# Soft-capped attention with a three-way max MLP: smaller token block, PSUM order, first loads and weight conversions changed

## The chip, the cores and the metric

The kernel runs on one core of a Trainium2 chip. The metric is the device time of one execution in microseconds; the time of the kernel before is the median of three runs. All rows below come from one further execution, recorded by the profiler.

## What is computed

Attention over 4 batches, 12 heads, 448 tokens and a head size of 64, with scores capped by a tanh, then an MLP over the 1792 tokens: three products with 768 x 768 matrices, their elementwise maximum, and a product with a fourth. All is float32; the reference, cut to its core:

```
def _attn_ref(q, k, v, cap):
    scale = 1.0 / np.sqrt(q.shape[-1])
    scores = scale * np.matmul(q, k.transpose(0, 1, 3, 2))
    scores = cap * np.tanh(scores / cap)
    scores = scores - np.max(scores, axis=-1, keepdims=True)
    attn = np.exp(scores)
    attn = attn / (np.sum(attn, axis=-1, keepdims=True) + 1e-09)
    return np.matmul(attn, v)

def _moe_ref(x, w1, w2, w3, w_out):
    h = np.maximum(np.maximum(x @ w1, x @ w2), x @ w3)
    return h @ w_out
```

## The kernel before

**Attention.** One group is four heads of one batch, so there are 12 groups, t = 0 to 11, and `step` is run for each of them and once more (t = 12) for what is left of the last. A group has 7 blocks of 64 keys, j = 0 to 6. For each block `scores` (L126) multiplies keys and queries into one of the two PSUM tiles `qk`, `tanh` (L132) and `expo` (L135) run on ScalarE into `e_all`, and `values` (L140) accumulates into PSUM tile `av`. With a cap of at most 40 no maximum is subtracted. The row sums are made by `add` on VectorE (s_t) and `sums` (L154) on TensorE into PSUM tile `sm`; `recip` (L161 to L164), `normalize` and `split_x` (L176, L177) on VectorE divide and write the result as a high and a low part into `xx`. A step begins with the sums of the group before it and ends with the first scores of the next one. All code stands in the order in which each engine runs it (a manual schedule); `FILL`, `CONV`, `SCALED` and `LOADS` say which extra work goes into which step.

**Weights.** The weights come as the 64-bit words of the host. Each of the 24 column strips n (18 of the first layer, three matrices for each of 6 output strips, and 6 of the second) is loaded by `conv_load` into `wd` and turned by the six operations of `conv` into a high and a low part, `wh` and `wl`. `CONV` names, by step, pairs of strip and operation that VectorE runs at the end of the step; `SCALED` names a step in which operation 0 is done by ScalarE; `LOADS` names the step in which a strip is loaded, by SP's queue.

**The MLP.** The tokens are cut into blocks, b = 0 of 256 tokens (`REST`) and b = 1 to 3 of 512. A unit (n, b) is one strip times one block: for each of 6 groups of 128 input features high x high, high x low and low x high are added up in one PSUM bank. For b = 0 the high weights take both parts of the 256 tokens in one product of 512 columns (L234), and a product of 256 columns adds the low weights (L235); `empty` then copies one half of the bank by ScalarE (L255) and adds the other by VectorE, and for the second and third matrix a further VectorE operation takes the maximum. For b = 1 to 3 three products of 512 columns are used (L239 to L241), and the bank is emptied by one operation. Eight units, those of `FILL`, stand inside the attention steps 4 to 11, in the bank `sm[:, 0]`: (0, 0), (1, 0), (2, 0) in steps 4, 5 and 6, then five with 512 tokens. The rest is done by `mlp` behind the attention, n by n and b by b. When the last strip of the first layer (n = 17) has been done for a block, `split_h` cuts the hidden values of this block into a high part (ScalarE, L276) and a low part (VectorE). `mlp` takes PSUM banks from the list `banks` in turn; the two halves of one PSUM tile are two banks. A strip has four units, so all its units of one parity are in `qk`, and all of the next strip's in `sm` and `av`:

```
banks = [t[:, i, :] for a, b in ((qk[0], qk[1]), (sm, av)) for i in range(2) for t in (a, b)]
```

**The start.** ScalarE's queue issues the cap (L441) and the first half of q (L443), SP's queue the first part of k, the second half of q, the rest of k, v and the first weights (L442 to L445, `load_v`, `conv_load`). Nine products of zeros (L450, `WARM`) run on TensorE meanwhile. The cap gives the scale of the tanh and a flag, on which all engines branch.

## Time and profile before

| | |
|---|---|
| median of 3 runs | 516.14 us (515.65 to 517.76) |
| profiled execution | 516.17 us |
| its span | 514.4 us |
| TensorE busy | 495.9 us, 96% of the span, 3073 products |
| VectorE, ScalarE busy | 269.0 us (52%), 233.3 us (45%) |
| steps 0 to 3 | to 61 us |
| steps 4 to 12 | 61 to 187 us |
| MLP behind the attention | 187 to 509.6 us |

The share of a busy engine over the whole span hides that different engines set the pace in different stages; so the profile is read stage by stage, and the row at which an engine starts again after a wait names what ended the wait. In the profile PE is TensorE, PEld its weight loads, DVE is VectorE, ACT is ScalarE, and a q behind a name is the engine's queue. L104 is a helper for VectorE's two-operand operations, so these are told apart by their tiles. A row of busy times gives the stretch and its length in us, then for PE, PEld, DVE, ACT and POOL the busy us and the instructions, then the granted TensorE clock as a share of 2.4 GHz, the busy share of the DMA engines and GB/s. A row of a timeline gives start and duration in us, engine, line, operation, tiles, shape and count; in brackets the idle time before it and what ended it.

### The profile page before, as it was taken

The numbers are of one execution on the slowest core, as the hardware profiler recorded it, in microseconds if no ns is written. First come the engines' busy times: TensorE is split into PE (matmuls) and PEld (weight loads), VectorE is DVE, ScalarE is ACT, GpSimd is POOL, SyncE is SP. The second block draws the span as 40 slices with busy tenths as digits, with TensorE's granted clock in tenths as the row PEclk, the third lists the DMA queues.
The fourth block names the chain that finished last, engine by engine and source line by source line (L and its number), as shares of the span: only waits on it lengthen the run. The fifth ranks groups of instructions, "written<-read, shape, count | busy, mean of one in ns | idle before, by whom it ended". The sixth has DMA issues, their size and how long they took to land.

```text
span 514.4 us, 7208 instructions
## 1 busy us (share of the span) xinstructions
PE 495.9 (96%) x3073; PEld 344.5 (67%) x3073; DVE 269.0 (52%) x355; ACT 233.3 (45%) x298; POOL 0.4 (0%) x6
## 2 busy tenths in 40 slices
PE   6899999989999999999999999999999997999996
PEld 3333344444455558888888888888888886888884
DVE  1798999986778963434324414423432585223100
ACT  5999999979788721311211121021022462222211
POOL 0000000000000000000000000000000000000000
PEclk9999999999999999999999999999999998999999
DMA  8234333412232100301301111210130101333111
GB/s 303 106 108 171 108 108 108 148 58 90 91 108 98 62 1 0 124 19 44 122 1 61 62 61 62 62 61 6 57 124 0 63 0 51 128 118 134 52 72 67
DMA packets 12710, 41.42 MB, mean 81 GB/s; under 512 B 1536, under 2 KB 2944, under 8 KB 12672
## 3 DMA queue, kind: packets, MB, share of 16 engines
q1 hardware_dynamic: 12240, 40.54, 22.8%
q8 instruction: 26, 0.43, 0.3%
q10 hardware_dynamic: 432, 0.36, 0.2%
q14 instruction: 12, 0.10, 0.1%
HBM read 35.39 MB, written 5.51 MB: 80 GB/s over the span
## 4 chain that ended last, share of the span: by engine, by line
PE 80%; DVE 10%; ACT 7%; issue 2%; DMA 1%; ACTq 0%; DVEq 0%
PE qk L239 9%; PE qk L240 9%; PE qk L241 9%; PE av L140 6%; PE qk L126 6%; PE av L239 6%; PE av L240 6%; PE av L241 6%; PE sm L239 4%; PE sm L241 4%; PE sm L240 4%; PE sm L234 4%; ACT e_all L132 3%; DVE s_t L104 3%; ACT e_all L135 3%; DVE xx L104 2%
## 5 line engine op out<-in xcount | busy, mean ns | idle before, releaser
L132 ACT ACTIVATE e_all<-qk,sc_t 128x896 f32<-128x896 f32 x84 | 83.3, 1006 | 13.1 <-PE qk L126 12.6
L135 ACT ACTIVATE e_all<-e_all,acap 128x896 f32<-128x896 f32 x84 | 86.5, 1046 | 0.5
L126 PE MATMUL qk<-q_t,k_t 64*64 64x448 f32 x672 | 78.6, 543 | 7.2 <-ACT e_all L132 6.1
L239 PE MATMUL qk<-xx,wh 128*128 128x512 f32 x204 | 80.4, 394 | 2.9 <-DVE q_t L104 2.9
L240 PE MATMUL qk<-xx,wh 128*128 128x512 f32 x204 | 80.0, 392 | 0.0
L241 PE MATMUL qk<-xx,wl 128*128 128x512 f32 x204 | 79.9, 392 | 0.0
L140 PE MATMUL av<-e_all,v_t 64*64 64x448 f32 x672 | 74.9, 536 | 0.3 <-DVE x_t L104 0.3
L104 DVE TENSOR_TENSOR s_t<-s_t,e_all 128x896 f32<-128x896 f32 x55 | 59.8, 1087 | 10.0 <-ACT e_all L135 7.7
L223 ACT CAST wh<-cw 128x768 fp32r<-128x768 f32 x21 | 17.6, 836 | 88.5 <-DVE cw L219 88.5
L126 PEld LDWEIGHTS qk<-q_t,k_t 64*64 64x64 f32 x672 | 23.4, 132 | 47.6 <-issue 24.1
L239 PE MATMUL av<-xx,wh 128*128 128x512 f32 x132 | 51.4, 390 | 0.0
L241 PE MATMUL av<-xx,wl 128*128 128x512 f32 x132 | 51.4, 389 | 0.0
L240 PE MATMUL av<-xx,wh 128*128 128x512 f32 x132 | 51.3, 389 | 0.0
L140 PEld LDWEIGHTS av<-e_all,v_t 64*64 64x64 f32 x672 | 25.4, 133 | 38.3 <-issue 35.4
L104 DVE TENSOR_TENSOR wl<-cw,wh 128x768 fp32r<-128x768 f32 x24 | 22.9, 955 | 47.3 <-ACT wh L223 39.8
L239 PEld LDWEIGHTS qk<-xx,wh 128*128 128x128 f32 x204 | 38.6, 189 | 12.2 <-DVE q_t L104 3.3
L241 PEld LDWEIGHTS qk<-xx,wl 128*128 128x128 f32 x204 | 38.7, 190 | 8.3
L240 PEld LDWEIGHTS qk<-xx,wh 128*128 128x128 f32 x204 | 38.7, 190 | 7.6
L239 PE MATMUL sm<-xx,wh 128*128 128x512 f32 x96 | 38.0, 395 | 0.0
L241 PE MATMUL sm<-xx,wl 128*128 128x512 f32 x96 | 37.4, 390 | 0.0
L240 PE MATMUL sm<-xx,wh 128*128 128x512 f32 x96 | 37.4, 389 | 0.0
L104 DVE TENSOR_TENSOR e_all<-e_all,qk 128x512 f32<-128x512 f32 (+1 forms) x17 | 11.2, 657 | 38.8 <-PE qk L241 36.8
(94 smaller groups left out, 552.1 us busy)
## 6 DMA issues: line engine op xcount, KB each, us to landing
wd<-in_wts_dram SPq DMA_DIRECT2D x24, 768.0 KB, 4.4
v_t<-in_v_dram SPq DMA_DIRECT2D x12, 448.0 KB, 3.3
k_t<-in_k_dram SPq DMA_DIRECT2D x11, 448.0 KB, 3.4
q_t<-in_q_dram SPq DMA_DIRECT2D x11, 448.0 KB, 4.7
out_dram<-q_t SPq DMA_DIRECT2D x6, 256.0 KB, 2.0
out_dram<-s_t SPq DMA_DIRECT2D x6, 256.0 KB, 2.0
out_dram<-x_t SPq DMA_DIRECT2D x5, 256.0 KB, 2.0
out_dram<-x_t SPq DMA_DIRECT2D x3, 128.0 KB, 2.2
```

What stands on the lines that cost most here:

```text
L104: eng.tensor_tensor(out=out, in0=in0, in1=in1, op=op)
L126: nc.tensor.matmul(ps[rows(s), R, 0:S], k_t[t % 2][rows(R), j, s, :], q_t[t % 2][rows(R), s, :], start=True, stop=True, skip_group_check=True,
L132: nc.scalar.activation(out=e_of(t, j), in_=slot(t, j)[:, :, 0:S], func=AF.Tanh, scale=sc_t)
L135: nc.scalar.activation(out=e_of(t, j), in_=e_of(t, j), func=AF.Exp, scale=acap)
L140: nc.tensor.matmul(av[rows(R), s, 0:S], v_t[t % 2][rows(s), j, R, :], e_of(t, j)[rows(s), R, :], start=(j == 0), stop=(j == NJ - 1), skip_ ...
L223: nc.scalar.copy(out=h, in_=d)
L234: nc.tensor.matmul(ps, w_h, xx[:, :, kc, at], start=(kc == 0), stop=False, skip_group_check=True)
L239: nc.tensor.matmul(ps, w_h, a_h, start=(kc == 0), stop=False)
L240: nc.tensor.matmul(ps, w_h, a_l, start=False, stop=False)
L241: nc.tensor.matmul(ps, w_l, a_h, start=False, stop=(kc == KC - 1))
```

## The change

- A unit of the 256-token block is made of three products of 256 columns, as the other blocks are of three of 512; both parts of `empty` for b = 0 become one operation: a copy by ScalarE for the first matrix and for the output, a maximum on VectorE for the second and third. The buffers `l_t` go.
- `banks` names the four PSUM tiles in turn, first their first halves, then their second.
- The conversions of the strips 0 to 2 move: those of one step are now in the step before it, or split in another way, the operation that ScalarE did in step 4 is done by VectorE in step 3, and strip 2 is loaded in step 1.
- The cap is stored as a column behind the first group's q. One load on ScalarE's queue brings both; behind it on the same queue come the rest of k, v and the first weights. SP's queue keeps the first part of k.
- Seven products of zeros stand at the start.

```diff
...
 CAP_LO = 1e-6
-WARM = 9
+WARM = 7
...
 BY_PE = (0, 1, 2, 3, 11)
-CONV = {1: [(0, 4), (0, 5)], 2: [(1, 0), (1, 1)], 3: [(1, 2), (1, 3)], 4: [(1, 4), (1, 5), (2, 1)],
-        5: [(2, 2), (2, 3), (2, 4), (2, 5)], 9: [(3, 1)], 10: [(3, 2), (3, 3)]}
-SCALED = {4: 2, 9: 3}
-LOADS = {0: 1, 2: 2, 6: 3, 11: 4}
+CONV = {0: [(0, 4), (0, 5)], 1: [(1, 0), (1, 1)], 2: [(1, 2), (1, 3)], 3: [(1, 4), (1, 5), (2, 0)],
+        4: [(2, 1), (2, 2)], 5: [(2, 3), (2, 4), (2, 5)], 9: [(3, 1)], 10: [(3, 2), (3, 3)]}
+SCALED = {9: 3}
+LOADS = {0: 1, 1: 2, 6: 3, 11: 4}
...
 @with_exitstack
-def attn_max_mlp_kernel(ctx: ExitStack, tc: tile.TileContext, q, k, v, cap, wts, out):
-
+def attn_max_mlp_kernel(ctx: ExitStack, tc: tile.TileContext, first, q, k, v, wts, out):
...
-    cap_t, acap, sc_t, eps_f, eps_g, fl = (
-        tl(n, [128, 1]) for n in ("cap_t", "acap", "sc_t", "eps_f", "eps_g", "fl")
-    )
+    acap, sc_t, eps_f, eps_g, fl = (tl(n, [128, 1]) for n in ("acap", "sc_t", "eps_f", "eps_g", "fl"))
     fl_i = tl("fl_i", [128, 1], I32)
...
-    q_t = ring("q_t", 2, [128, 2, S])
+    q_0 = tl("q_0", [128, 2 * S + 8])
+    q_t = [q_0[:, 0:2 * S].rearrange("p (a b) -> p a b", a=2), tl("q_1", [128, 2, S])]
+    cap_t = q_0[:, 2 * S:2 * S + 1]
     k_t = ring("k_t", 2, [128, NJ, 2, 64])
...
     m_0 = tl("m_0", [128, TOK])
-    l_t = ring("l_t", 2, [128, REST])
     wd = ring("wd", 2, [128, KC * 128, 2], I32)
...
     o_t = [flat(t)[:, 0:512] for t in (*q_t, *s_t, *x_t)]
-    banks = [t[:, i, :] for a, b in ((qk[0], qk[1]), (sm, av)) for i in range(2) for t in (a, b)]
+    banks = [t[:, i, :] for i in range(2) for t in (qk[0], qk[1], sm, av)]
...
         nc.sync.dma_start(out=quarters(k_t[t % 2]), in_=k[t])
-        nc.sync.dma_start(out=flat(q_t[t % 2]), in_=q[t])
-
-    def load_v(t):
-        nc.sync.dma_start(out=quarters(v_t[t % 2]), in_=v[t])
+        nc.sync.dma_start(out=flat(q_t[t % 2]), in_=q[t - 1])
+
+    def load_v(t, queue=nc.sync):
+        queue.dma_start(out=quarters(v_t[t % 2]), in_=v[t])
...
-    def conv_load(n):
-        nc.sync.dma_start(out=flat(wd[n % 2]), in_=wts[n].bitcast(I32))
+    def conv_load(n, queue=nc.sync):
+        queue.dma_start(out=flat(wd[n % 2]), in_=wts[n].bitcast(I32))
...
         at = slice(*BLOCKS[b])
+        ps = ps[:, 0:at.stop - at.start]
         for kc in kcs:
             w_h, w_l, a_h, a_l = wh[n % 3][:, kc, :], wl[n % 3][:, kc, :], xx[:, 0, kc, at], xx[:, 1, kc, at]
-            if b == 0:
-                nc.tensor.matmul(ps, w_h, xx[:, :, kc, at], start=(kc == 0), stop=False, skip_group_check=True)
-                nc.tensor.matmul(
-                    ps[:, 0:REST], w_l, a_h, start=False, stop=(kc == KC - 1), skip_group_check=True
-                )
-                continue
             nc.tensor.matmul(ps, w_h, a_h, start=(kc == 0), stop=False)
...
         at = slice(*BLOCKS[b])
-        if n >= 3 * KC:
-            dst = out[n - 3 * KC][:, at]
-            o = o_t[outs[0] % len(o_t)][:, 0:dst.shape[1]]
-            outs[0] += 1
-        else:
-            o = m_t[f][:, at] if w == 0 else l_t[n % 2]
-        if b == 0:
-            nc.scalar.copy(out=o, in_=ps[:, 0:REST])
-            tt(nc.vector, o, o, ps[:, REST:2 * REST], ALU.add)
-            if n < 3 * KC and w:
-                tt(nc.vector, m_t[f][:, at], m_t[f][:, at], o, ALU.max)
-        elif n < 3 * KC and w:
-            tt(nc.vector, m_t[f][:, at], m_t[f][:, at], ps, ALU.max)
-        elif (n, b) == (NU - 1, NB - 1):
+        ps = ps[:, 0:at.stop - at.start]
+        if n < 3 * KC:
+            m = m_t[f][:, at]
+            if w == 0:
+                nc.scalar.copy(out=m, in_=ps)
+            else:
+                tt(nc.vector, m, m, ps, ALU.max)
+            return
+        dst = out[n - 3 * KC][:, at]
+        o = o_t[outs[0] % len(o_t)][:, 0:at.stop - at.start]
+        outs[0] += 1
+        if (n, b) == (NU - 1, NB - 1):
             one, two = slice(0, 256), slice(256, 512)
...
             nc.scalar.dma_start(out=dst[:, two], in_=o[:, two])
-            return
         else:
             nc.scalar.copy(out=o, in_=ps)
-        if n >= 3 * KC:
             nc.sync.dma_start(out=dst, in_=o)
...
     with tc.manual_schedule():
-        nc.scalar.dma_start(out=cap_t, in_=cap.partition_broadcast(128))
         nc.sync.dma_start(out=k_t[0][:, 0:2].rearrange("p a b c -> p (a b c)"), in_=k[0, :, 0:256])
-        nc.scalar.dma_start(out=q_t[0][:, 0], in_=q[0, :, 0:S])
-        nc.sync.dma_start(out=q_t[0][:, 1], in_=q[0, :, S:2 * S])
-        nc.sync.dma_start(out=k_t[0][:, 2:].rearrange("p a b c -> p (a b c)"), in_=k[0, :, 256:])
-        load_v(0)
-        conv_load(0)
+        nc.scalar.dma_start(out=q_0[:, 0:2 * S + 1], in_=first)
+        nc.scalar.dma_start(out=k_t[0][:, 2:].rearrange("p a b c -> p (a b c)"), in_=k[0, :, 256:])
+        load_v(0, nc.scalar)
+        conv_load(0, nc.scalar)
         nc.vector.memset(wz.bitcast(F32), 0.0)
...
-_INS = ["q", "k", "v", "cap", "wts"]
+_INS = ["first", "q", "k", "v", "wts"]
...
     host = {
-        "q": qq.reshape(NG, 128, 2 * S),
+        "first": _np.concatenate(
+            [qq[0, 0].reshape(128, 2 * S), _np.broadcast_to(_np.asarray(inputs["cap"]).reshape(1, 1), (128, 1))], axis=1
+        ),
+        "q": qq.reshape(NG, 128, 2 * S)[1:],
         "k": kk.reshape(NG, 128, 2 * S),
         "v": vv.reshape(NG, 128, 2 * S),
-        "cap": _np.asarray(inputs["cap"]).reshape(1),
         "wts": _np.concatenate([w_in.reshape(18, 128, KC * 128), w_out.reshape(6, 128, KC * 128)]).view(_np.int64),
...
```

What the order of instructions becomes is shown at three places. ScalarE at its start (DMA rows are the loads that its queue issues), before:

```order
L441 DMA cap_t_61<-in_cap_dram 128x1
L443 DMA q_t0_70<-in_q_dram 128x448
L453 ACT_TABLE_LOAD
L453 ACTIVATE acap_62<-cap_t_61 128x1
L460 ACTIVATE eps_f_64<-acap_62 128x1
L132 ACTIVATE e_all_76<-qk0_100,sc_t_63 128x896
```

And after:

```order
L431 DMA q_0_69<-in_first_dram 128x897
L432 DMA k_t0_71<-in_k_dram 128x640
L112 DMA v_t0_73<-in_v_dram 128x896
L198 DMA wd0_84<-in_wts_dram 128x1536
L440 ACT_TABLE_LOAD
L440 ACTIVATE acap_61<-q_0_69 128x1
L447 ACTIVATE eps_f_63<-acap_61 128x1
L130 ACTIVATE e_all_75<-qk0_97,sc_t_62 128x896
```

The load of q stands first, with the cap in it, and three loads that SP's queue had issued stand behind it, ahead of the table load.

VectorE from the unit of step 5 to the sums of step 6 (s_t is the running sum of exponents, x_t the reciprocal, cw, wh and wl belong to the conversion, m_0 is the running maximum of the MLP), before:

```order
L104 TENSOR_TENSOR l_t1_86<-l_t1_86,sm_102 128x256
L104 TENSOR_TENSOR m_0_84<-m_0_84,l_t1_86 128x256
L104 TENSOR_TENSOR s_t1_78<-s_t1_78,e_all_76 128x896 x4
L215 SCALAR_TENSOR_TENSOR cw0_89<-wd0_87,cw0_89 128x768
L219 SCALAR_TENSOR_TENSOR cw0_89<-wd0_87,cw0_89 128x768
L225 CAST wh2_93<-cw0_89 128x768
L104 TENSOR_TENSOR wl2_96<-cw0_89,wh2_93 128x768
L161 STREAM_TRANSPOSE x_t1_80<-sm_102 128x896
```

And after:

```order
L102 TENSOR_TENSOR m_0_83<-m_0_83,sm_99 128x256
L102 TENSOR_TENSOR s_t1_77<-s_t1_77,e_all_75 128x896 x4
L217 SCALAR_TENSOR_TENSOR cw0_86<-wd0_84,cw0_86 128x768
L223 CAST wh2_90<-cw0_86 128x768
L102 TENSOR_TENSOR wl2_93<-cw0_86,wh2_90 128x768
L159 STREAM_TRANSPOSE x_t1_79<-sm_99 128x896
```

Two operations are gone ahead of the reciprocal of step 6: the add that joined the two halves of the unit, and one step of the conversion, which now stands a step earlier.

TensorE at the start of the second layer, the last three products of unit (18, 1) and the first three of (18, 2), with the semaphores that each waits for (Activation is ScalarE; xx holds the hidden values), before:

```order
L239 MATMUL qk1_101<-xx_83,wh0_91 128x512 [waits Activation_49]
L240 MATMUL qk1_101<-xx_83,wh0_91 128x512 [waits DVE_49]
L241 MATMUL qk1_101<-xx_83,wl0_94 128x512
L239 MATMUL qk0_100<-xx_83,wh0_91 128x512 [waits DVE_49]
L240 MATMUL qk0_100<-xx_83,wh0_91 128x512
L241 MATMUL qk0_100<-xx_83,wl0_94 128x512
```

And after:

```order
L232 MATMUL qk1_98<-xx_82,wh0_88 128x512 [waits Activation_49]
L233 MATMUL qk1_98<-xx_82,wh0_88 128x512 [waits DVE_49]
L234 MATMUL qk1_98<-xx_82,wl0_91 128x512
L232 MATMUL sm_99<-xx_82,wh0_88 128x512 [waits DVE_49,Activation_49]
L233 MATMUL sm_99<-xx_82,wh0_88 128x512 [waits DVE_49]
L234 MATMUL sm_99<-xx_82,wl0_91 128x512
```

Unit (18, 2) goes to `sm` and not back to `qk0`; its products wait one by one for the parts of xx, where before one wait at its head stood for all of them.

## Rows read from the trace of the kernel before

**Rows 1.** Busy time by stretch: step 3, step 6, the MLP.

```profile
47.95:61.00 13.05, 12.28 (x136) 4.73 (x132) 11.64 (x15) 12.92 (x16) 0.00 (x0) 1.00 0.33 110
...
89.84:106.05 16.21, 14.21 (x132) 6.13 (x132) 15.64 (x19) 15.38 (x18) 0.00 (x0) 1.00 0.38 134
...
186.65:514.40 327.75, 320.07 (x1462) 265.94 (x1458) 118.22 (x174) 70.86 (x120) 0.00 (x0) 0.99 0.18 61
```

**Rows 2.** TensorE's timeline, steps 5 and 6: start, duration, instruction, wait.

```profile
75.60 0.93 PE L154 MATMUL sm<-s_t,ones 64*64 64x448 f32 x8
...
88.59 0.97 PE L126 MATMUL qk<-q_t,k_t 64*64 64x448 f32 x8
89.84 0.98 PE L154 MATMUL sm<-s_t,ones 64*64 64x448 f32 x8 [0.28 <-DVE s_t L104]
...
106.05 0.98 PE L154 MATMUL sm<-s_t,ones 64*64 64x448 f32 x8 [1.73 <-DVE s_t L104]
```

**Rows 3.** TensorE's timeline at the start of the second layer.

```profile
418.51 0.39 PE L234 MATMUL qk<-xx,wh 128*128 128x512 f32 x1
...
424.48 0.39 PE L241 MATMUL qk<-xx,wl 128*128 128x512 f32 x1
427.77 0.50 PE L239 MATMUL qk<-xx,wh 128*128 128x512 f32 x1 [2.90 <-DVE q_t L104]
...
433.59 0.39 PE L239 MATMUL qk<-xx,wh 128*128 128x512 f32 x1
```

**Rows 4.** Busy time by stretch as in rows 1, one microsecond behind the hole.

```profile
430.00:431.00 1.00, 1.00 (x4) 0.81 (x3) 0.18 (x1) 0.00 (x0) 0.00 (x0) 0.50 0.00 0
```

**Rows 5.** VectorE's timeline, the low halves of block 3.

```profile
424.30 3.09 DVE L104 TENSOR_TENSOR xx<-e_all,xx 128x512 fp32r<-128x512 f32 x5
```

**Rows 6.** Instruction groups by form: count, busy us, mean ns, idle.

```profile
L104 DVE TENSOR_TENSOR wl<-cw,wh 128x768 fp32r<-128x768 f32 x24 | 22.9, 955 | 47.3 <-ACT wh L223 39.8 <-PE qk L241 7.5
L215 DVE SCALAR_TENSOR_TENSOR cw<-wd,cw 128x768 int32<-128x768 int32 x24 | 22.9, 955 | 0.3
...
L225 DVE CAST wh<-cw 128x768 fp32r<-128x768 f32 x3 | 1.7, 555 | 0.0
```

**Rows 7.** VectorE's timeline, emptying the unit of step 5.

```profile
84.39 0.41 DVE L104 TENSOR_TENSOR l_t<-l_t,sm 128x256 f32<-128x256 f32 x1
```

**Rows 8.** VectorE's timeline, the reciprocal at the start of step 4.

```profile
62.70 1.12 DVE L161 STREAM_TRANSPOSE x_t<-sm 128x896 f32<-128x896 f32 x1 [0.23 <-PE sm L154]
```

**Rows 9.** TensorE's timeline, unit (17, 0) and the next one's start.

```profile
404.15 0.39 PE L234 MATMUL sm<-xx,wh 128*128 128x512 f32 x1
404.38 0.28 PE L235 MATMUL sm<-xx,wl 128*128 128x256 f32 x1
404.49 0.40 PE L234 MATMUL sm<-xx,wh 128*128 128x512 f32 x1
...
406.26 0.40 PE L239 MATMUL av<-xx,wh 128*128 128x512 f32 x1
```

**Rows 10.** Timeline of the weight loads in unit (0, 0).

```profile
67.01 0.19 PEld L234 LDWEIGHTS sm<-xx,wh 128*128 128x128 f32 x1
...
67.12 0.19 PEld L235 LDWEIGHTS sm<-xx,wl 128*128 128x128 f32 x1
```

**Rows 11.** Timeline of all engines at the start.

```profile
0.73 0.41 ACTq L441 DMA_DIRECT2D cap_t<-in_cap_dram  x1
...
1.17 0.45 ACTq L443 DMA_DIRECT2D q_t<-in_q_dram  x1
...
1.38 3.73 PE L450 MATMUL sm<-wz 128*128 128x448 f32 x9 [1.38 <-DVE wz L448]
...
6.16 1.73 PE L126 MATMUL qk<-q_t,k_t 64*64 64x448 f32 x16 [1.05 <-DMA q_t<-in_q_dram]
```

**Rows 12.** Loads by issue: engine, count, KB each, us from issue to landing.

```profile
q_t<-in_q_dram ACTq DMA_DIRECT2D x1, 224.0 KB, 4.9
...
cap_t<-in_cap_dram ACTq DMA_DIRECT2D x1, 0.5 KB, 3.6
```

## The prediction, made before the changed kernel ran

> **What bounds the kernel now.** I read the busy times by stretch first, to learn which engine each stage waits for, then the timeline of that engine where the stage is longer than its work. Three regimes show. In the first attention steps (t = 0 to 3) ScalarE is busy all the time, 12.92 of 13.05 us in step 3, and VectorE has slack (11.64 us) [rows 1]. In steps 4 to 6 a first-layer unit is put into each step and VectorE fills up, 15.64 of 16.21 us in step 6 [rows 1]. From step 7 on TensorE runs without a gap, and in the MLP it is busy for 320.07 of 327.75 us [rows 1]; what it lacks there is one hole and the tail after its last product.
>
> The loss in steps 5 and 6 is read from where the row sums of one step follow those of the next [rows 2]. Step 5 starts its sums at 75.60; its last score group starts at 88.59, and the sums could follow 0.80 later, so a step with nothing missing takes 88.59 + 0.80 - 75.60 = 13.79 us. It took 14.24, the next one 106.05 - 89.84 = 16.21. Both times the releaser is VectorE's s_t: 0.45 + 2.42 = 2.87 us lost.
>
> The hole in the MLP lies where the second layer begins [rows 3]. The last product before it starts at 424.48, its successor could start 0.23 later, at 424.71, and starts at 427.77, released by VectorE's q_t. That is the add that empties unit (18, 0), out of PSUM tile qk0; the waiting unit (18, 2) takes the other half of the same tile. After the hole the granted clock falls to 0.50, the 1.2 GHz level [rows 4]. Unit (18, 3) starts at 433.59; without the hole it would have been 424.71 + 18 x 0.2269 = 428.79 (a unit is 18 products; from 406.26 to 418.51 three units run, 12.25 / 54 = 0.2269) [rows 3, 9]. The loss is 4.80 us, idle time and slow clock together.
>
> **The change part by part.** The sum is made against the profiled execution, 516.17 us, whose span is 514.4; the median of the runs shown is 516.14, so the same sum serves both.
>
> *Four PSUM tiles in turn.* In the new order of banks a unit meets its tile again four units later, not two. Unit (18, 2) then takes sm, last used by (17, 2), and (18, 0) is emptied by ScalarE alone. What it still waits for are its own inputs, the split halves of block 2; VectorE is at the last five low halves of block 3 from 424.30 on, so those of block 2 are done before that [rows 5]. What is late next is unit (18, 3): its last low half ends at 424.30 + 3.09 = 427.39, and TensorE would be there at 428.79, a margin of 1.40 us. So the hole closes and, with no idle time ahead of it, I expect no slow clock: **4.8 us gained**; between 4.0, if the margin is eaten in part, and 4.8.
>
> *VectorE in steps 4 to 6.* Conversion steps move forward by one step. Step 4 gives away a cast (0.555) and a low half (0.955) and gets one of 0.955 back: 0.56 less. Step 5 gives away 0.96 [rows 6]. Emptying a 256-token unit costs VectorE an add of 0.41 and, for the units of steps 5 and 6, a max of like length before [rows 7]; the new form is nothing for the unit of step 4 (a copy by ScalarE alone, 0.41 less) and one max for those of steps 5 and 6 (0.41 less each). In all 0.56 + 0.41 + 0.96 + 0.41 + 0.41 = 2.75 us of VectorE's work leave three steps in which it has no gaps. Part of the 0.97 of step 4 only becomes a wait, since there the last exponent comes just ahead of the add. The lower bound is 1.78 (steps 5 and 6 alone), the upper the 2.87 that TensorE lost; I take about the middle, **2.35 us**, which leaves TensorE about half a us short of closing the gap in step 6. ScalarE also loses the conversion of step 4 and two copies; it is not late there, so that is worth nothing by itself.
>
> *Where the conversions go.* Steps 0 to 3 are ScalarE's; VectorE's fullest of them is step 3. The tightest place is the start of step 4: VectorE waits 0.23 us for the sums there [rows 8], and the conversions ahead of that wait grow from 2 x 0.955 to 0.955 + 0.555 + a scaling that I put at the cast's 0.555, by 0.16 us. That fits and costs nothing; with the cover gone it would be 0.16. Moving the load of weight 2 a step forward puts 768 KB ahead of the next k and q on SP's queue; both have their first reader a whole step later. Nothing.
>
> *Three products of 256 columns.* Per 128 input features the old pair takes (406.26 - 404.15) / 6 = 0.352 us; in the six pairs the product of 512 columns holds the engine for 0.23 to 0.24 us, mean 0.235, and that of 256 for 0.11 to 0.12, mean 0.117 [rows 9]. The new form is three of 256: 3 x 0.117 = 0.351. The doubtful part is the weight load, now three where there were two. The record of one is 0.19 us long, longer than the product, but two of them start 0.11 apart [rows 10], so they overlap, and the 0.117 already holds a product whose successor loads its own weights meanwhile. No row shows three in succession. If the cost of a column is what the 512-column products show (0.2269 / 512 x 256 = 0.1135), three are 0.340; if all of their excess over 512 columns at 2.4 GHz (0.2269 - 0.2133 = 0.0136) is paid by each product, 0.361. Over 24 units x 6 groups that is from 1.6 us gained to 1.3 lost; I take the 0.351, the nearest row, **0.1 us gained**.
>
> *The start.* The queue of ScalarE carries the cap before the first half of q, so q is issued at 1.17 and lands 4.9 us later; the scores start at 6.16 [rows 11, 12]. In the new order q with the cap as its last column is issued first, at 0.73, and k's first part is the only other load that the first scores need; the rest follows on ScalarE's queue behind q. The nearest rows bound the landing: the cap alone took 3.6 us from 0.73, so 4.33, and q's own 4.9 gives 5.6 [rows 12]. I take 5.0, between them, since fewer bytes are ahead of q than before: scores at 5.15, **1.0 us gained**, from 0.45 to 1.7. The scale for the first tanh needs a few tiny VectorE operations behind the cap; they run beside the first scores. Steps 0 to 3 are ScalarE's without a gap, so this moves everything behind it.
> By the rows alone that is a choice between two ends, and a rule speaks for the poorer one. The Trainium skill ("Trainium Kernel Development and Optimization", Key Constraints) says that all queues share the same 16 DMA engines and that issuing from several engines saves only issue time. By it the start gives just the 0.45 us, and the sum would end at 508.5.
>
> The two warm-up products taken out are off the path as long as q lands after the others. They run 0.41 us apart, 3.73 for nine [rows 11], for 448 columns, a slower pace than the 0.227 of 512 columns later. If with seven the first scores still run at that pace, the first 8 take 1.5 instead of 0.75 us: up to 0.75 lost, taken at nothing.
>
> The sum: 4.8 + 2.35 + 0.1 + 1.0 = 8.25 us; 516.17 - 8.25 = **507.9 us**.
>
> **The rivals.** *The weight loads set the pace (slower than before).* If three products of 256 in succession each need the full 0.19 us of a weight load, a group is 0.57 instead of 0.352, 144 times: 31 us lost, against 8.15 gained elsewhere: 539 us. It would decide from a product of (0.352 + 8.15 / 144) / 3 = 0.136 us on. For it speaks the length of the record, and that in the old pair the mean distance of two loads is 0.176, not far below it. Against it: two of three overlap by 0.08 us in every pair without falling behind. Chance 0.05.
>
> *The hole stays under another name.* If unit (18, 2) or (18, 3) waits for its halves, or for an emptying that the new order makes late, as long as it did for qk0, the 4.8 is not gained: 512.7 us. For it: VectorE is busy throughout this place. Against it: the halves are done 1.4 us before TensorE comes. Chance 0.08.
>
> *The start gives nothing.* The queue lands q hardly earlier and the scores run at the slow pace: 0.45 - 0.75 = -0.3 instead of +1.0, so 509.2 us; with the lower bound in steps 4 to 6, 509.8. Chance 0.12.
>
> **How the numbers follow.** The forecast has 0.75. The ends of the terms, from good to bad: 4.8 to 4.0, 2.87 to 1.78, +1.6 to -1.3, 1.7 to -0.3, so 505.2 to 512.0 if all fell to one side, which they do not. The range is 505.5 to 511.0: it takes in the third rival and leaves out the other two and the worst corner. This kernel's measurement tells about 0.5%, 2.6 us. Faster by more than that: the forecast, the third rival and most of the second, 0.91; within it 0.04; slower only by the weight loads, 0.05.
>
> **What would show it.** In the profile after: no idle time of TensorE at the start of the second layer and clock 1.00 there; steps 5 and 6 near 13.8 and 14.3 us, with VectorE's s_t still the releaser in step 6 for about half a us; units of 256 tokens at 2.1 us; scores at about 5.1 us. Wrong would be units of 256 near 3 us, a new wait for xx in unit (18, 3), or scores not before 5.6.

## The result and the profile after

The changed kernel takes 510.18 us (median of 4 runs, 509.52 to 511.02) where the kernel before takes 516.13 (515.65 to 517.76): ratio 0.988, 95% interval 0.9852 to 0.9908. In a later series, beside some of the experiments below, it took 509.66 beside 516.44, ratio 0.9852 (0.9818 to 0.9887). The forecast was 507.9, its range 505.5 to 511.0: the sign and the range held, the gain was 6 to 7 us and not 8.25. The profiled execution took 509.67 us with a span of 507.9, so the two profiles differ by 6.5 us. That is the difference taken apart here.

The start, answering [rows 11, 12]: timeline of the first 8 us, then the load's row (KB, us from issue to landing).

```profile
0.73 0.41 ACTq L431 DMA_DIRECT2D q<-in_first_dram  x1
...
1.38 2.98 PE L437 MATMUL sm<-wz 128*128 128x448 f32 x7 [1.38 <-DVE wz L435]
...
5.18 1.74 PE L124 MATMUL qk<-q,k_t 64*64 64x448 f32 x16 [0.82 <-DMA q<-in_first_dram]
...
q<-in_first_dram ACTq DMA_DIRECT2D x1, 448.5 KB, 4.4
```

The scores start at 5.18 in place of 6.16, 0.98 us earlier: 0.44 from the issue, the rest because the load landed in 4.4 us where the old one took 4.9, although it carries twice the bytes.

The sums of steps 3 to 8, answering [rows 2], and VectorE ahead of those of step 7, answering [rows 7].

```profile
46.96 0.93 PE L152 MATMUL sm<-s_t,ones 64*64 64x448 f32 x8
...
59.99 0.93 PE L152 MATMUL sm<-s_t,ones 64*64 64x448 f32 x8
...
74.57 0.93 PE L152 MATMUL sm<-s_t,ones 64*64 64x448 f32 x8
...
88.39 0.93 PE L152 MATMUL sm<-s_t,ones 64*64 64x448 f32 x8
...
102.95 0.98 PE L152 MATMUL sm<-s_t,ones 64*64 64x448 f32 x8 [0.54 <-DVE s_t L102]
...
118.80 0.93 PE L152 MATMUL sm<-s_t,ones 64*64 64x448 f32 x8
```

```profile
97.89 0.42 DVE L102 TENSOR_TENSOR m<-m,sm 128x256 f32<-128x256 f32 x1
98.22 4.67 DVE L102 TENSOR_TENSOR s_t<-s_t,e_all 128x896 f32<-128x896 f32 x4
```

Step 5 takes 88.39 - 74.57 = 13.82 us (14.24 before), step 6 14.56 (16.21). Ahead of the running sum VectorE now has one maximum for the unit, where an add and a maximum stood. Of the waits of 0.28 and 1.73 us one of 0.54 is left.

TensorE at the start of the second layer, answering [rows 3, 4, 9]: the first products of units (18, 0) to (19, 0); then busy time from unit (18, 2) to (19, 0), and VectorE's last five low halves of block 3, answering [rows 5].

```profile
416.28 0.28 PE L232 MATMUL qk<-xx,wh 128*128 128x256 f32 x1
...
418.43 0.40 PE L232 MATMUL qk<-xx,wh 128*128 128x512 f32 x1
...
422.54 0.39 PE L232 MATMUL sm<-xx,wh 128*128 128x512 f32 x1
...
426.62 0.39 PE L232 MATMUL av<-xx,wh 128*128 128x512 f32 x1
...
430.70 0.28 PE L232 MATMUL qk<-xx,wh 128*128 128x256 f32 x1
```

```profile
422.54:430.70 8.16, 8.16 (x38) 6.76 (x36) 5.97 (x9) 2.52 (x4) 0.00 (x0) 1.00 0.22 80
```

```profile
422.07 3.09 DVE L102 TENSOR_TENSOR xx<-e_all,xx 128x512 fp32r<-128x512 f32 x5
```

No wait is left, TensorE is busy for 8.16 of 8.16 us, and the granted clock is 1.00, the 2.4 GHz level. From the first product of unit (18, 0) to that of (18, 3) it takes 426.62 - 416.28 = 10.34 us where it took 15.08 (418.51 to 433.59, [rows 3]): the 4.8 us are there, but for the 0.06 that the new units cost. Unit (18, 0), three products of 256 columns for each group of features, takes 418.43 - 416.28 = 2.15 us, where the old pairs took 2.11, and the four units of a strip 430.70 - 416.28 = 14.42, where they took 14.36 (404.15 to 418.51, [rows 9, 3]). Of these 0.06 us, 0.04 lie in the unit itself and 0.02 in the one behind it, which takes 422.54 - 418.43 = 4.11 where the one behind the old pairs took 4.09 (406.26 to 410.35); why was not tried. Over 21 strips behind the attention that is 21 x 0.06 = 1.3 us lost.

The ledger: start 0.98, steps 4 to 6 2.14 (steps 4 to 7 together 60.96 to 58.81), hole 4.8, products -1.3; 6.6 us, against 6.5 measured.

### The profile page after: what moved, and what is told of

It reads as the page before. It is cut to its first block, busy times and chain, and to the rows that moved or that the text cites. A ratio compares the mean times of both kernels' runs of the same rounds, so it can differ in the third digit from the quotient of the medians.

```text
span 507.9 us, 7474 instructions
## 1 busy us (share of the span) xinstructions
PE 494.1 (97%) x3215; PEld 350.7 (69%) x3215; DVE 259.8 (51%) x332; ACT 229.3 (45%) x285; POOL 0.4 (0%) x6
## 3 DMA queue, kind: packets, MB, share of 16 engines
q10 hardware_dynamic: 720, 2.16, 1.1%
HBM read 35.39 MB, written 5.51 MB: 81 GB/s over the span
## 4 chain that ended last, share of the span: by engine, by line
PE 88%; ACT 6%; DVE 3%; issue 1%; DMA 1%; ACTq 0%; DVEq 0%
PE qk L232 9%; PE qk L233 9%; PE qk L234 9%; PE qk L124 9%; PE av L138 8%; PE sm L232 8%; PE sm L234 8%; PE sm L233 8%; PE av L234 6%; PE av L232 6%; PE av L233 6%; ACT e_all L130 3%; ACT e_all L133 3%; PE sm L152 3%; DVE s_t L102 1%
## 5 line engine op out<-in xcount | busy, mean ns | idle before, releaser
L232 PE MATMUL qk<-xx,wh 128*128 128x512 f32 (+1 forms) x264 | 89.6, 339 | 0.0
L233 PE MATMUL qk<-xx,wh 128*128 128x512 f32 (+1 forms) x264 | 89.6, 339 | 0.0
L234 PE MATMUL qk<-xx,wl 128*128 128x512 f32 (+1 forms) x264 | 89.3, 338 | 0.0
L124 PE MATMUL qk<-q,k_t 64*64 64x448 f32 x672 | 78.7, 543 | 7.0 <-ACT e_all L130 6.2
L232 PE MATMUL sm<-xx,wh 128*128 128x512 f32 (+1 forms) x180 | 69.0, 383 | 0.0
L234 PE MATMUL sm<-xx,wl 128*128 128x512 f32 (+1 forms) x180 | 68.2, 379 | 0.0
L233 PE MATMUL sm<-xx,wh 128*128 128x512 f32 (+1 forms) x180 | 68.1, 378 | 0.0
L124 PEld LDWEIGHTS qk<-q,k_t 64*64 64x64 f32 x672 | 23.2, 132 | 47.1 <-ACT e_all L130 21.5
L232 PEld LDWEIGHTS qk<-xx,wh 128*128 128x128 f32 x264 | 50.1, 190 | 6.3 <-issue 0.7
L234 PEld LDWEIGHTS qk<-xx,wl 128*128 128x128 f32 x264 | 50.0, 189 | 5.6
L233 PEld LDWEIGHTS qk<-xx,wh 128*128 128x128 f32 x264 | 50.1, 190 | 5.4
L232 PEld LDWEIGHTS sm<-xx,wh 128*128 128x128 f32 x180 | 33.8, 188 | 11.7 <-DVE x_t L162 4.9
```

What stands on the lines that cost most here:

```text
L124: nc.tensor.matmul(ps[rows(s), R, 0:S], k_t[t % 2][rows(R), j, s, :], q_t[t % 2][rows(R), s, :], start=True, stop=True, skip_group_check=True,
L232: nc.tensor.matmul(ps, w_h, a_h, start=(kc == 0), stop=False)
L233: nc.tensor.matmul(ps, w_h, a_l, start=False, stop=False)
L234: nc.tensor.matmul(ps, w_l, a_h, start=False, stop=(kc == KC - 1))
```

## The experiments

A short name stands for each kernel. They ran in three series, each on one chip beside the kernel before: e1 to e4; e5, e6, e7 and the changed kernel once more; e9 to e12.

**Which part closes the hole.** Three kernels take the change apart.

The kernel before with the new list alone:

```
-    banks = [t[:, i, :] for a, b in ((qk[0], qk[1]), (sm, av)) for i in range(2) for t in (a, b)]
+    banks = [t[:, i, :] for i in range(2) for t in (qk[0], qk[1], sm, av)]
```

> The kernel before with the new list of banks alone; the 256-token units keep their pair of products and the add by VectorE. Theory A (the hole at the start of the second layer closes because unit (18, 2) no longer meets the tile of (18, 0)): no wait of TensorE there, 4.8 us less, 511.3 us. Theory B (it closes because (18, 0) is emptied by ScalarE alone): the list does nothing, 516.1 us.

Measured 512.61 us (511.63 to 512.69) beside 517.42, ratio 0.9899 (0.9882 to 0.9916). In its timeline TensorE's unit (18, 2), then VectorE's add for (18, 0):

```profile
425.90 0.39 PE L239 MATMUL sm<-xx,wh 128*128 128x512 f32 x1
...
428.50 0.42 DVE L104 TENSOR_TENSOR q_t<-q_t,qk 128x256 f32<-128x256 f32 x1
```

The add still comes 2.6 us after the unit's start, but in another PSUM tile, so nobody waits for it. The list alone closes the hole. (In the old list all four units of strip 18 lie in `qk0` and `qk1`, (18, 0) and (18, 2) in the two halves of `qk0`.) This kernel lies 4.8 us below the kernel before beside it. Its profiled execution, 512.66, lies only 3.5 below that of the kernel before, since its sums of step 4 came at 62.18 in place of 60.95; the start, which the list does not touch, differs from execution to execution (see the zeros below).

The changed kernel with the old list (the diff above, reversed):

> The changed kernel with the old list of banks. Theory A: the hole of 2.9 us and the slow clock behind it come back, 510.2 + 4.8 = 515.0 us. Theory B: unit (18, 0) is emptied by ScalarE before TensorE needs the tile, no hole, 510.2 us. If the list alone also closes it (first run of this set), either part is enough by itself.

Measured 509.78 us (509.63 to 510.07) beside 517.42, ratio 0.985 (0.9833 to 0.9866). ScalarE's copy for (18, 0), then unit (18, 2) at TensorE:

```profile
422.34 0.36 ACT L259 COPY q<-qk 128x256 f32<-128x256 f32 x1
...
424.26 0.39 PE L232 MATMUL qk<-xx,wh 128*128 128x512 f32 x1
```

The unit meets the other half of `qk0` again, but its emptying is now one copy that is over 1.5 us before. So the list isn't needed beside the new emptying.

The kernel before with the new products and `empty` alone:

```
-            if b == 0:
-                nc.tensor.matmul(ps, w_h, xx[:, :, kc, at], start=(kc == 0), stop=False, skip_group_check=True)
...
-                continue
...
-        if b == 0:
-            nc.scalar.copy(out=o, in_=ps[:, 0:REST])
-            tt(nc.vector, o, o, ps[:, REST:2 * REST], ALU.add)
```

> The kernel before with the new 256-token units alone (three products of 256 columns, one operation to empty the bank), old banks, old conversions, old start. Theory B: hole closed (-4.8), about 1 us from VectorE in steps 5 and 6, and 21 units in the MLP that are each 0.06 us longer (+1.3): 511.6 us. Theory A: the hole stays: 516.4 us. In both the period of one strip in the MLP is 14.42 us instead of 14.36.

Measured 512.29 us (511.45 to 513.83) beside 517.42, ratio 0.9909 (0.9888 to 0.993), no wait at the second layer, a strip in 14.45 us (418.25 to 432.70). Its sums of steps 5 to 7:

```profile
75.28 0.93 PE L154 MATMUL sm<-s_t,ones 64*64 64x448 f32 x8
...
89.10 0.93 PE L154 MATMUL sm<-s_t,ones 64*64 64x448 f32 x8
...
104.84 0.98 PE L154 MATMUL sm<-s_t,ones 64*64 64x448 f32 x8 [1.34 <-DVE s_t L104]
```

One VectorE operation less per unit gives 0.42 in step 5 and 0.47 in step 6. Each of the two parts closes the hole by itself; together they do it once.

**The conversions alone.** The kernel before with the new `CONV`, `SCALED` and `LOADS`:

> The kernel before with the new places of the conversions and the earlier load alone. 0.56 us of VectorE's work leave step 4 and 0.96 step 5; by the sum of the prediction's term, without the part of the units, 0.96 to 1.5 us less in steps 4 to 6: 514.6 to 515.2 us; the hole stays. If the conversions only collide with the reciprocals of steps 1 to 4, nothing is gained: 516.1 us.

Measured 516.02 us (513.26 to 517.23, 8 runs) beside 517.42, ratio 0.9973 (0.9946 to 1.0): by the times alone a gain of 1.4 us, hardly told from nothing. TensorE's waits (us in total, times, longest), then one microsecond behind the hole:

```profile
PE qk L239 <- DVE q_t L104: 2.9, 1, 2.9
...
PE sm L154 <- DVE s_t L104: 1.2, 1, 1.2
...
430.00:431.00 1.00, 1.00 (x4) 0.79 (x3) 0.00 (x0) 0.00 (x0) 0.00 (x0) 0.50 0.00 0
```

The hole and the clock of 0.50 behind it are as before, as expected; step 5 takes 13.91 (75.90 to 89.81) and step 6 15.23 (to 105.04), 0.33 and 0.98 less than before. Units and conversions together would give 0.75 and 1.45 in steps 5 and 6; the change gives 0.42 and 1.65, since step 5 has no more than its 0.45 to give.

**The start alone, and the changed kernel once more.** `first` with the cap behind q, its place in ScalarE's queue, and seven products of zeros, in the kernel before:

```
-        nc.scalar.dma_start(out=cap_t, in_=cap.partition_broadcast(128))
...
-        nc.scalar.dma_start(out=q_t[0][:, 0], in_=q[0, :, 0:S])
...
+        nc.scalar.dma_start(out=q_0[:, 0:2 * S + 1], in_=first)
...
```

> The kernel before with only the start of the changed one (q with the cap as its last column first on ScalarE's queue, the rest of k, v and the first weights behind it, seven products of zeros). Theory A (the start's 1.0 us is a gain of its own, since ScalarE sets the pace of steps 0 to 3 and passes it on): the scores start at 5.1 to 5.2 us, the sums of step 4 near 60.0, and the kernel is 1.0 us faster than the kernel before. Theory B (it is given back where VectorE is full, in steps 4 to 6): the sums of step 4 come 1.0 earlier, those of step 7 not, and the kernel is within 0.3 us of the kernel before. By the Trainium skill's rule on queues it would be 0.45 us faster. The hole at the second layer stays in all of them.

Measured 515.78 us (513.91 to 517.21, 10 runs) beside 516.44, ratio 0.9969 (0.9949 to 0.9989). Its first scores and its sums of steps 4 and 8:

```profile
4.64 2.72 PE L125 MATMUL qk<-q,k_t 64*64 64x448 f32 x16 [0.28 <-DMA q<-in_first_dram]
...
60.30 0.93 PE L153 MATMUL sm<-s_t,ones 64*64 64x448 f32 x8
...
121.30 0.93 PE L153 MATMUL sm<-s_t,ones 64*64 64x448 f32 x8
```

q arrives 1.5 us before that of the kernel before, but the 16 products take 2.72 in place of 1.73, and the gain is 0.65 at step 4 (before: 60.95) and still 0.61 at step 8 (before: 121.91). It is passed on, as theory A has it. Its size, 0.66 us by the medians, lies between the 0.45 and the 1.0 of the expectation; in this execution the pace of the first products took part of it back.

> The changed kernel once more, beside the three others of this call, as their common base: 509.5 to 511.0 us, as in its first runs. Theory A on the start (the pace of the first scores differs from execution to execution): its times fall into more than one group, about a microsecond apart. Theory B (the start is the same in each execution and the spread has another source): the profile again shows the first 16 score products from 5.1 to 5.3 us on in 1.7 us.

Measured 509.66 us (509.17 to 510.03): no second group in these four runs. The first scores in its profile:

```profile
4.78 2.16 PE L124 MATMUL qk<-q,k_t 64*64 64x448 f32 x16 [0.42 <-DMA q<-in_first_dram]
```

The 16 products start at 4.78 and take 2.16, and the sums of step 4 come at 60.00, as in the first profile (59.99): q lands earlier, the pace is lower, and both come out alike. The pace does differ from execution to execution, which is theory A's premise, but the two groups of times that it expected are not there; theory B's mark is missed too. So this run left the spread of the times open.

**The zeros.** The changed kernel with `WARM = 9`, and with `WARM = 2`:

> The changed kernel with nine products of zeros ahead of the scores in place of seven. In the profiles with seven the first 16 score products took 1.73 to 2.72 us, from 4.6 to 5.2 us on. Theory A (uninterrupted products ahead of the scores bring TensorE to its full pace): the zeros end at 5.11, the scores follow without idle time and take 1.73, first tanh at 6.0 to 6.1, median up to 0.3 us below that of the changed kernel, spread under 0.6 us. Theory B (the moment at which the pace rises is not set by them): the 16 take up to 2.5 us again, median 509.5 to 510.2, spread of a microsecond.

> The changed kernel with two products of zeros ahead of the scores in place of seven, so TensorE idles from 2.2 us to the landing of q near 4.8. Theory A (the products ahead of the scores set their pace): the first 16 score products and more run at half the pace, 3.4 us, the first tanh comes at 6.6 to 7.4 in place of 6.0 to 6.6, and the kernel is 0.5 to 2 us slower than the changed one. Theory B (they do nothing): 1.7 to 2.7 us for the first 16, 509.2 to 511.0 as the changed kernel.

Measured 509.52 us (509.33 to 510.65) with nine and, on the same chip, 510.60 (510.45 to 510.73) with two, beside 516.41. The zeros and the first scores, of nine and then of two, and of two the busy times of two stretches as in [rows 1]:

```profile
1.38 3.73 PE L437 MATMUL sm<-wz 128*128 128x448 f32 x9 [1.38 <-DVE wz L435]
5.04 4.94 PE L124 MATMUL qk<-q,k_t 64*64 64x448 f32 x32
```

```profile
1.38 1.12 PE L437 MATMUL sm<-wz 128*128 128x448 f32 x2 [1.38 <-DVE wz L435]
...
4.65 5.57 PE L124 MATMUL qk<-q,k_t 64*64 64x448 f32 x32 [2.15 <-DMA q<-in_first_dram]
...
1.40:4.30 2.90, 1.09 (x2) 0.48 (x2) 0.00 (x0) 1.28 (x1) 0.00 (x0) 1.00 0.82 254
4.70:8.00 3.30, 3.30 (x20) 1.14 (x24) 0.60 (x5) 1.36 (x4) 0.00 (x0) 1.00 1.02 417
```

With two, 32 products take 5.57 us, and by the medians the kernel is 1.1 us slower than with nine and 0.9 slower than with seven (509.66 in its own series): theory A. With nine they follow without a gap and yet take 4.94 in that execution (510.65, the slowest of its four and as slow as those with two), against theory A; the spread is that of theory B, and the median fits both. So some of the zeros are worth about a microsecond by the medians, but two more than seven are worth nothing that these runs tell.

The moment from which the pace is full stands in the traces, though in none of the rows above. A trace keeps the granted clock as records, each with its start and its level, and a stretch that has no record is printed as 1.00. The first record, at the full level, begins at these times (us from the start of the span):

| kernels | first clock record |
|---|---|
| nine zeros, then a gap (e4, before, e3, e1) | 4.88, 5.30, 5.51, 10.53 |
| nine zeros without a gap (e11) | 7.28 |
| seven zeros (after, e7, e10, e9, after_again, e2, e6, e5) | 4.59, 5.14, 5.60, 5.62, 5.69, 6.35, 6.50, 6.69 |
| two zeros (e12) | 9.41 |

Ahead of it four score products take 0.75 to 0.80 us, behind it 0.38 to 0.43, in all 14 profiles. So the 16 products took 1.74 in the first profile of the changed kernel because the record there, 4.59, begins before the scores at 5.18, and 2.72 in e5, where it begins at 6.69. This also moves the sums of step 4: from 60.58 to 62.18 in the four profiles with the old start and nine zeros, from 59.78 to 60.36 in the eight with the new start and seven. What sets the moment stays open: with nine zeros alone it lies anywhere from 4.88 to 10.53, past the one value with two.

**What a product costs.** Three widths, read from the timeline. First, each product of 256 columns cut into two of 128:

```
-            nc.tensor.matmul(ps, w_h, a_h, start=(kc == 0), stop=False)
...
+            for c in ((0, 128), (128, 256)) if b == 0 else ((0, size),):
+                p, tk = ps[:, c[0]:c[1]], slice(at.start + c[0], at.start + c[1])
...
```

> The changed kernel with each product of 256 columns of the 256-token block cut into two of 128 columns, so 36 products for a unit in place of 18, each with its own weight load. Theory A (every product pays the same excess, about 0.013 us, over its columns at 2.4 GHz): a product of 128 takes 0.0533 + 0.013 = 0.066 us, a unit 2.39 in place of 2.15, and 24 units cost 5.8 us: about 516.0. Theory B (the weight load sets the pace as soon as a product is shorter than it; two loads were seen 0.11 us apart): 0.11 for each, 3.96 for a unit, 43 us more: about 553. Theory C (cost goes by columns alone): no change, about 510.2.

Measured 554.96 us (554.67 to 555.42), ratio 1.0733 (1.0695 to 1.077). One unit of 36 products, to the first product of the next, and the busy times of about this stretch:

```profile
400.76 0.22 PE L237 MATMUL qk<-xx,wh 128*128 128x128 f32 x1
...
404.73 0.45 PE L237 MATMUL qk<-xx,wh 128*128 128x512 f32 x1
...
401.00:405.00 4.00, 4.00 (x36) 3.97 (x36) 1.52 (x2) 0.07 (x1) 0.00 (x0) 1.00 0.25 104
```

3.97 / 36 = 0.110 us each: theory B. Columns at 2.4 GHz would be 0.0533, and the granted clock is 1.00. The weight loads are busy for 3.97 of 4.00 us and start 0.11 apart (400.87, 400.98, 401.09), as two were seen to [rows 10]. That it is the load that sets this pace, and not another cost of each load and product together, is argued: no run has products of 128 columns that share a load. By the Trainium skill ("TensorE: Matmul & The Clock Gate", LDWEIGHTS) a load takes its columns over 1.2 GHz, by which we estimate 0.107 us for 128; the trace's 0.110 agrees.

Then 384 columns in the 15 units of 256 tokens in the MLP's first layer:

```
-        at = slice(*BLOCKS[b])
+        at = slice(BLOCKS[b][0], BLOCKS[b][1] + more)
...
```

> The changed kernel with each product of the 256-token block widened to 384 columns in the 15 such units of the MLP's first layer (the added 128 columns are computed and not used). What a product takes is then read at a third width. Theory A (each product pays the same excess over its columns, so the line through 0.1194 us at 256 and 0.2269 at 512 holds): 0.173 us, a unit 3.12, period of four strips' units 15.39, and the kernel 14.5 us longer, 524.2. Theory B (a column costs what the 512-column products show, 0.443 ns, and only the 256-column products are held up, by the weight loads that stand 0.110 apart with 128 columns): 0.170, a unit 3.06, period 15.33, 13.6 us longer, 523.3.

Measured 524.62 us in its one run; unit (17, 0), and the next strip:

```profile
400.48 0.33 PE L232 MATMUL qk<-xx,wh 128*128 128x384 f32 x1
...
403.62 0.39 PE L232 MATMUL qk<-xx,wh 128*128 128x512 f32 x1
...
415.90 0.33 PE L232 MATMUL qk<-xx,wh 128*128 128x384 f32 x1
```

A product is (403.62 - 400.48) / 18 = 0.174, a strip 15.42: theory A, by these rows. Over the columns at 2.4 GHz a product pays 0.0127 us at 256 (0.1194 - 0.1067), 0.0144 at 384, 0.0136 at 512: about the same for each at these three widths.

Last, the changed kernel with the old pair for the 256-token units of the MLP alone:

```
+            if pair:
+                nc.tensor.matmul(whole, w_h, xx[:, :, kc, at], start=(kc == 0), stop=False, skip_group_check=True)
+                nc.tensor.matmul(ps, w_l, a_h, start=False, stop=(kc == KC - 1), skip_group_check=True)
+                continue
...
```

> The changed kernel with the old pair of products (512 columns, then 256) and the old two-part emptying for the 256-token units of the MLP alone; the three units inside the attention steps stay three products of 256. Theory A (the third product costs 0.06 us for each unit, as the two profiles say): 21 units, 1.3 us faster than the changed kernel, about 508.9, and units of 256 tokens 4 strips apart by 14.36 us again. Theory B (the difference lies in something else that the profiles mix in): within 0.4 us of the changed kernel. In both the hole at the second layer stays closed, since the four PSUM tiles still go round; were it back, the time would be about 513.7.

Measured 509.07 us (508.22 to 510.42), 0.6 below the changed kernel beside it, which four runs can't tell from nothing. The rows can: a unit's first and second product, the next unit's first, and that of the next strip.

```profile
415.14 0.39 PE L235 MATMUL qk<-xx,wh 128*128 128x512 f32 x1
415.37 0.28 PE L236 MATMUL qk<-xx,wl 128*128 128x256 f32 x1
...
417.25 0.40 PE L238 MATMUL qk<-xx,wh 128*128 128x512 f32 x1
...
429.50 0.39 PE L235 MATMUL qk<-xx,wh 128*128 128x512 f32 x1
```

Unit 2.11, strip 14.36, as before the change, and the second layer starts without a wait. From the start of the MLP to its last product it takes 317.79 us (183.28 to 501.07) against 319.05 (183.48 to 502.53): 1.26 less, theory A.

**A faster version.** The pairs in the MLP, and the conversions a little further forward:

```
-CONV = {0: [(0, 4), (0, 5)], 1: [(1, 0), (1, 1)], 2: [(1, 2), (1, 3)], 3: [(1, 4), (1, 5), (2, 0)],
-        4: [(2, 1), (2, 2)], 5: [(2, 3), (2, 4), (2, 5)], 9: [(3, 1)], 10: [(3, 2), (3, 3)]}
+CONV = {0: [(0, 4), (0, 5)], 1: [(1, 0), (1, 1), (1, 2)], 2: [(1, 3), (1, 4), (1, 5)], 3: [(2, 0), (2, 1), (2, 2)],
+        4: [(2, 3), (2, 4)], 5: [(2, 5)], 9: [(3, 1)], 10: [(3, 2), (3, 3)]}
...
```

> The changed kernel with two edits: the old pair of products and two-part emptying for the 256-token units of the MLP alone, and the conversions of strips 1 and 2 one or two operations further forward in steps 1 to 5 (three in each of steps 1 to 3, two in step 4, one in step 5). Theory A (in step 6 TensorE's last 0.54 us of waiting for s_t is VectorE's work of steps 4 and 5, and ScalarE, not VectorE, is the bound of steps 1 to 3): no wait for s_t is left, sums of step 6 at 102.4 and of step 7 at 118.2 with those of step 4 unchanged near 60.0; with the pairs, which give 1.3 to 1.6, about 1.8 us faster than the changed kernel, 508.0. Theory B (VectorE's slack in steps 1 to 3 is too small for three operations): the sums of step 4 come 0.3 or more later and the half us is only moved, 508.4 to 508.8.

Measured 507.72 us (507.58 to 509.33, 5 runs) beside 516.41, ratio 0.9836 (0.9817 to 0.9855); the changed kernel was at 0.9852 to 0.988. The sums of steps 7 and 8 (in the expectation 6 and 7):

```profile
102.27 0.93 PE L153 MATMUL sm<-s_t,ones 64*64 64x448 f32 x8
...
118.09 0.93 PE L153 MATMUL sm<-s_t,ones 64*64 64x448 f32 x8
```

The last wait for s_t is gone and the sums come 0.68 earlier than in the changed kernel, with those of step 4 unmoved (60.00): theory A. With the pairs this has the lowest median of the kernels run, some 2 us below the changed one. That one did not run in the same series; its variant with nine zeros did and took 509.52, 1.8 more.

## Why the prediction was right, and where it was off

**The hole: right in size and in cause, but a cause too few.** 4.8 us came as predicted, with clock 1.00. The next one late was to be unit (18, 3), with 1.40 us to spare; VectorE ends its halves at 422.07 + 3.09 = 425.16 and TensorE comes at 426.62, 1.46. What the working put down to the new list was enough, as e1 shows, but the single copy by ScalarE, which it named in passing, is also enough, as e2 and e3 show. Only undoing the parts one at a time told this; the trace after can't.

**VectorE in steps 4 to 6: right.** 2.14 against 2.35, with 0.54 left of the "about half a us". Steps 5 and 6 were to take near 13.8 and 14.3 and took 13.82 and 14.56.

**New places of the conversions: right.** Step 3 takes 59.99 - 46.96 = 13.03 us as before. There was even room for one operation more in steps 1 and 2, which e9 used.

**The products: this term failed.** The working took 3 x 0.117 from the distance at which a 512-column product follows a short one in the pair, and came to 0.1 us gained; 1.3 were lost. The mechanism at the far end of its range, each product paying the same 0.013 or so over its columns, is the one that the widths show: three short ones pay it three times, 0.358 a group. That is 0.04 us a unit, 0.9 of the 1.3; the other 0.4 are the 0.02 in the unit behind, for which the working had no term. It was the term with no row for what the change does, three short products in succession, and "the nearest row" was a short product between two long ones. It is nearly the whole miss: 8.25 less 1.4 for it and 0.2 for VectorE is 6.65.

**The weight loads** were rightly left at 0.05, with a bound that held: 0.119 us per product lies under the 0.136 from which they decide. But the rival is real one size lower. At 128 columns a pace of 0.110, that of the loads' starts and not their records' length of 0.19, costs 45 us.

**The start: right, with luck.** Scores at 5.18 against 5.15, and 0.96 us of it are left at the sums of step 4. The Trainium skill's rule ("Trainium Kernel Development and Optimization", Key Constraints), by which only the issue's 0.45 is saved, was too poor here: the load also landed in 4.4 us in place of 4.9, and in the other profiles of the new start the scores began from 4.63 to 5.04. Measurement decides; whether the cap's load ahead of it or the half of q on SP's queue had held it up was not tried. The hit on 5.15 is luck: the first profile has the latest landing of the ten, and the one of them in which the first scores found the full pace. Where q came sooner, the low pace took part of it back, and the sums of step 4 lie between 59.78 and 60.36 in the eight profiles with seven zeros. The working put that pace at nothing, with up to 0.75 us as its price; in e5 it cost 2.72 - 1.74 = 0.98. Its 0.41 us between zeros, 3.73 over nine, counts the end of the last one in: in the traces they start 0.373 apart from the second on, the 1.2 GHz level for 448 columns. The two zeros less cost nothing that these runs tell; e12, by its median, shows that five less than that would.

## What to carry to other kernels

Price a changed form of work by a row that has this form in succession; where none exists, as with three short products here, test the fixed cost per instruction first, since splitting work pays it again. Where an engine waits for the emptying of a PSUM tile, both a shorter emptying and a longer round of tiles can be enough, and one of them is free to be given up again (here the third product was). An engine that is full in one stage gets its gain from operations moved to stages that another engine bounds, step by step until its wait is gone.

## What the runs showed of the hardware

- **A weight load's pace and its record differ.** For 128x128 weights at clock 1.00 the record is 0.19 us long whatever the width of the product behind it; in the units of 128 columns the loads follow each other every 0.110 us. So products of 256 columns (0.119) run just above that pace, and those of 128 (0.110) at it.
- **The first products run at the low level, and a printed clock of 1.00 does not tell it.** From the second on the zeros start 0.373 us apart in every profile with more than two of them, which is 448 columns at 1.2 GHz, and four score products take 0.75 to 0.80 us until the first clock record begins, about half that behind it. The stretches before that record are printed as 1.00 because they have none. With the same seven zeros the record began from 4.59 to 6.69 us and the first 16 score products took 1.74 to 2.72 us in eight executions. So ahead of the first record the distance of the products tells the level, not the printed clock.
- **The low clock behind one and the same hole has no fixed length.** After the wait of 2.9 us the records at 0.50 last 3.41 us in the profiles of the kernel before (from 428.55) and of e4, and 6.83 in that of e5 (426.53 to 433.35), whose execution, 517.21 us, is the slowest of its ten. At half the clock 3.41 us more cost, as an estimate, 1.7. That this is what spreads the times of the kernel before was not shown: kernels without the hole spread too (e3 from 511.45 to 513.83, e7 from 508.22 to 510.42).
- **What a low clock costs depends on where it falls.** Behind the hole 3.41 us at 0.50 cost 1.7, the 4.80 less the 3.06 from 424.71 to 427.77. In e7 the clock is at 0.50 from 11.96 to 15.38 us, where ScalarE is busy without a gap and TensorE for 3.10 of 3.42 us, and from the 17th score product to the sums of step 1 it takes 13.60 us (7.08 to 20.68), as in the changed kernel (7.29 to 20.89): nothing lost. In e4 it is at 0.50 from 15.12 to 18.53, TensorE is busy for all of it, and that stretch takes 14.14 (8.11 to 22.25), 0.54 more.
